# First unit's keys, queries and values evicted straight into attention's places

## The chip, the cores and the metric

The kernel runs on one core of one Trainium2 chip. The metric is the device time of one execution in microseconds (us); a kernel's time is the median of its runs.

## What is computed

The reference mixes two branches of the same 2048 x 640 input `x` in float32, with one gate per row:

```python
g = sigmoid((x * gate_w).sum(-1, keepdims=True))
qkv = x @ wqkv                   # 32 heads of 20, for q, k and v
idx = pos[:, None] - 2 * arange(8)[None, :]          # keys s, s-2, ..., s-14
logits = einsum("bhsd,bhswd->bhsw", q, k[idx]) * scale   # masked where idx < 0
a = (softmax(logits) applied to v[idx]) @ wo
b = irfft2(rfft2(x) * (w_r + 1j * w_i))
out = g * a + (1 - g) * b
```

The attention is local and dilated: row s looks at itself and at the seven rows before it with a step of two.

## The kernel before, in words

**Layout.** Row s of the input stands in partition s // 16 at place j = s % 16. Rows of even j and of odd j never meet in the attention, so the work has two parities (`par`), each with eight places `jj` (j = 2 jj + par). Eight consecutive places of one parity are in one partition, and the seven older keys that the first places need are in the partition in front. Columns are in four groups `hg` of 480: q, k and v of 160 columns each, and each of these in two halves `f` of 80 (`HC`, four heads of 20). A **unit** is u = 4 par + hg; one attention call `attend(par, h)` does half a unit, h = 2 hg + f.

**Projection** (`qkv`, lines 1038 to 1057). For each of the 64 combinations of place and group, fifteen matmuls (five blocks of 128 input columns, three terms of a high and low split) fill one PSUM bank with 480 columns; there are four such banks. Unit 0's first place has no split and takes five slower matmuls. ScalarE copies each bank into a tile `ev` (two places per tile), and each pair of places goes to a DRAM scratch `qkvd` (`store_rows`, line 1001). Units 0 and 4 store from SyncE's queue (SP), the others from ScalarE's. In the scratch, the rows of one column half are consecutive over all partitions.

**Attention** (`attend`, lines 1080 to 1115). `fetch` (line 1067) reads per half unit 15 consecutive key rows per partition into `kt` (seven of the partition in front, eight own), and eight query rows into `q`; `attend` reads the 15 value rows into `vt`. For units 0 and 4 all of these are on SP. Then, for each pair of places, `products` (line 1170) multiplies 2 x 8 x 80 elements of `kt` and `q` into `pr` and sums them in groups of 20 into the logits `L`. The multiplication is VectorE's, with the query first copied by ScalarE into a PSUM bank (`qbank`), except for some pairs that GpSimd does (`POOL_PR`; none in unit 0). Masks, maximum, exponential (ScalarE) and sums follow; GpSimd subtracts, scales and does the weighted products `pv`; VectorE reduces them to `o`, which goes to a second scratch `od`. `weigh`, `mask` and the rings of places `kv0` to `kv5`, `q0` to `q1`, `L0` to `L2`, `pr0`, `pr1` are shared by all half units. Unit 0's `ev` tiles use `ev0`, `ev1`, `pr0`, `pr1`.

**The rest.** Columns of `x` are folded (`fold`, on VectorE or GpSimd; folds 3 to 6 use the places `pv0`, `pv1` and are stored to DRAM), transformed by matmuls (`cols`, tiles `z`), multiplied in the frequency domain (`freq`, tiles a to d, `xa`, `xc`, `P`, `g`), transformed back (`spatial`, tiles oa to od, `ha`, `hb`); the output projection is `project_even` and `project_odd` (`woa`, `wob`, fifteen matmuls each). The low halves of the projection weights (`w<-raw,w`) and of the odd rows of `x` (`xo<-xt,xo`) are subtracted on GpSimd.

**What sets the order.** The program records all operations (`Plan.record`; every instruction is issued from one helper, so the trace gives it line 987) and orders them before anything is issued: a list schedule over estimated costs is repeated once per number in `STEPS`, each of which seeds random moves, and the list `MOVES` then takes single operations out of an engine's order and puts them at another place. Each engine and each DMA queue issues in that order. Units are taken in the order `UNITS` = (0,0), (0,1), (1,0), (1,1), (0,2), and so on, as (parity, half). `work` (line 857) records the stages.

Of the kernel before, what the change touches and what calls it, by code (L numbers as in the profile page):

```python
# [18 lines left out]
HD = 20  # L19
GORD = (1, 2, 3, 4, 5, 0) + tuple(range(6, 16))  # L20
GC = 160
HC = 80
# [127 lines left out]
class Plan:  # L150
# [394 lines left out]
)  # L545
MOVES = (
# [1085 lines left out]
```

## Time and profile before

| | us |
|---|---|
| median of 3 runs (lowest, highest) | 441.99 (441.64, 442.71) |
| the profiled execution | 443.3 |
| its span, from the first instruction to the last | 441.5 |
| TensorE, VectorE, GpSimd, ScalarE busy in the span | 428.1, 380.6, 353.5, 209.3 |

All is one profiled execution. A matmul's recorded end is modelled, and matmuls overlap, so a busy TensorE need not run at its peak. TensorE's clock was granted in full over the whole span. An idle stretch of an engine is put down to what it waited for last.

### The profile page before, as it was taken

Reading aid. Unit: us, or ns where it says so; the run is one execution under the profiler, and the core shown is the slowest. Engines: PE = TensorE matmul, PEld = TensorE weight load, DVE = VectorE, ACT = ScalarE, POOL = GpSimd, SP = SyncE. Lnnn points to the kernel's source line nnn. Section 1 sums busy time; section 2 is a strip of 40 time slices with the busy share of each in tenths; the row PEclk is TensorE's granted clock in tenths of the full one; section 3 lists DMA queues with packets and bytes.
Section 4 is the critical chain, followed back from the end, with each engine's and each line's share of the span. In section 5 each row is a group of like instructions: output and inputs, shape, how many; then the busy total and the mean of one; then the engine's idle time right before and its main releaser. Section 6 shows DMA issues by size and latency. Waiting matters only on the chain.

```text
span 441.5 us, 9185 instructions
## 1 busy us (share of the span) xinstructions
PE 428.1 (97%) x3501; PEld 372.5 (84%) x3501; DVE 380.6 (86%) x499; ACT 209.3 (47%) x551; POOL 353.5 (80%) x313
## 2 busy tenths in 40 slices
PE   4999999999999999999999999999999999999996
PEld 3788888888888888888888778798889899999996
DVE  2575089899999999999999999999999999989682
ACT  3574245242225223453235466666766876754310
POOL 1067876589999999798799967887488999876994
PEclk9999999999999999999999999999999999999999
DMA  8959998929676658999588677957843445443545
GB/s 296 379 172 344 333 351 276 355 80 322 199 204 210 186 162 223 322 303 305 180 244 240 193 235 256 314 193 250 313 136 91 117 118 149 76 58 112 148 91 117
DMA packets 83835, 95.52 MB, mean 216 GB/s; under 512 B 18104, under 2 KB 73528, under 8 KB 83792
## 3 DMA queue, kind: packets, MB, share of 16 engines
q1 hardware_dynamic: 53728, 68.39, 47.9%
q10 hardware_dynamic: 28848, 23.85, 18.0%
q0 software_dynamic: 1216, 2.71, 4.5%
q8 instruction: 27, 0.44, 0.4%
q14 instruction: 16, 0.13, 0.1%
HBM read 64.04 MB, written 30.89 MB: 215 GB/s over the span
## 4 chain that ended last, share of the span: by engine, by line
PE 78%; DVE 10%; DMA 4%; ACT 3%; issue 2%; POOL 1%; SPq 0%; ACTq 0%; DVEq 0%; POOLq 0%
PE qkv L987 44%; PE woa L987 7%; PE wob L987 7%; PE a L987 4%; PE g L987 3%; PE oa L987 2%; PE xa L987 2%; PE oTp L987 2%; DMA kt3a<-qkvd 2%; PE hb L987 2%; PE xc L987 1%; POOL pv6b L987 1%; DMA qkvd<-ev 1%; DVE o2a L987 1%; DVE pr3a L987 1%
## 5 line engine op out<-in xcount | busy, mean ns | idle before, releaser
L987 PE MATMUL qkv<-w,xo 128*128 128x480 f32 (+1 forms) x480 | 115.7, 386 | 0.7 <-ACT ev L987 0.7
L987 PE MATMUL qkv<-w,xe 128*128 128x480 f32 (+1 forms) x465 | 107.3, 382 | 0.0
L987 PEld LDWEIGHTS qkv<-w,xo 128*128 128x128 f32 x480 | 89.1, 188 | 18.1 <-ACT ev L987 2.4
L987 PEld LDWEIGHTS qkv<-w,xe 128*128 128x128 f32 x465 | 87.4, 188 | 14.8 <-ACT ev L987 0.6
L987 ACT COPY ev<-qkv 128x480 f32<-128x480 f32 x64 | 35.4, 562 | 74.6 <-PE qkv L987 67.9
L987 PE MATMUL woa<-wo,oT 128*128 128x320 f32 x240 | 44.5, 321 | 0.5 <-DVE oT L987 0.5
L987 PE MATMUL wob<-wo,oT 128*128 128x320 f32 x240 | 43.3, 319 | 0.0
L987 PEld LDWEIGHTS woa<-wo,oT 128*128 128x128 f32 x240 | 36.8, 188 | 2.2 <-DVE oT L987 1.4
L987 PEld LDWEIGHTS wob<-wo,oT 128*128 128x128 f32 x240 | 36.6, 188 | 1.4 <-ACT ya L987 0.4
L987 POOL TENSOR_TENSOR P<-X,wp 128x642 f32<-128x642 f32 x16 | 25.1, 1568 | 12.0 <-ACT X L987 12.0
L987 POOL TENSOR_TENSOR xo<-xt,xo 128x640 fp32r<-128x640 f32 x8 | 12.4, 1571 | 23.2 <-ACT z L987 23.2
L987 PEld LDWEIGHTS a<-bt,zg 32*128 32x128 f32 x160 | 22.1, 184 | 2.7 <-issue 1.7
L987 PE MATMUL a<-bt,zg 32*128 32x161 f32 x160 | 24.1, 300 | 0.0
L987 PE MATMUL b<-bt,zg 32*128 32x161 f32 x160 | 24.1, 300 | 0.0
L987 PE MATMUL d<-bt,zg 32*128 32x161 f32 x160 | 24.1, 300 | 0.0
L987 PE MATMUL c<-bt,zg 32*128 32x161 f32 x160 | 24.1, 300 | 0.0
L987 PE MATMUL oa<-gt,zj 32*128 32x160 f32 x160 | 24.0, 300 | 0.0
L987 PE MATMUL ob<-gt,zj 32*128 32x160 f32 x160 | 24.0, 300 | 0.0
L987 PE MATMUL oc<-gt,zj 32*128 32x160 f32 x160 | 23.8, 299 | 0.0
L987 PE MATMUL od<-gt,zj 32*128 32x160 f32 x160 | 23.8, 299 | 0.0
L987 PEld LDWEIGHTS oa<-gt,zj 32*128 32x128 f32 x160 | 21.9, 185 | 1.4 <-issue 1.1
L987 PEld LDWEIGHTS b<-bt,zg 32*128 32x128 f32 x160 | 22.1, 184 | 0.0
(303 smaller groups left out, 1246.8 us busy)
## 6 DMA issues: line engine op xcount, KB each, us to landing
qkvd<-ev ACTq DMA_DIRECT2D x24, 480.0 KB, 3.7
wp<-in_ws SPq DMA_DIRECT2D x16, 642.0 KB, 5.6
fx<-in_x SPq DMA_DIRECT2D x8, 640.0 KB, 6.9
qkvd<-ev SPq DMA_DIRECT2D x8, 480.0 KB, 5.9
raw<-in_wqkv SPq DMA_DIRECT2D x15, 240.0 KB, 4.1
xt<-in_xT SPq DMA_DIRECT2D x8, 320.0 KB, 8.4
fd<-fx SPq DMA_DIRECT2D x4, 640.0 KB, 6.6
mm<-in_t_mm SPq DMA_DIRECT2D x8, 320.0 KB, 3.8
```

The lines of the kernel that those rows point to most:

```text
L987: p.sp.dma_start(raw[:, c0:c1], src[:, c0:c1])
```

## The change

Unit 0 (`par` 0, `hg` 0) no longer goes through the scratch.

- `own` takes both halves' places `kt`, `vt`, `q` and `L` at the start and clears the seven front rows of partition 0 on VectorE.
- `keep` takes the place of the eviction: six copies of 80 columns per bank, straight to row 7 + jj of `kt` and `vt` and row jj of `q`. ScalarE makes four (values' come as numbers 4 and 5, on VectorE).
- After each second place it records products of the pair with the keys that are there in the partition itself: rows 7 - m to 7, that is 1, 3, 5 and 7 of 8 rows, for m = 0, 2, 4 and 6. For m = 2 and 4 GpSimd multiplies; VectorE does all reductions.
- After the last place, rows 8 to 14 of `kt` and `vt` go to rows 0 to 6 of the next partition by transfers within the on-chip memory, each in two pieces (112 and 15 partitions): eight transfers on SP.
- `attend` for the two halves fetches nothing and does the other 7, 5, 3 and 1 rows of the products, all on VectorE.
- Four stores and six fetches are gone. Unit 0's tiles `ev` are gone, and with them its use of `pr0` and `pr1` as such.
- `first_keys`, which nothing called, and the unused parameters `block`, `c0` are taken out.
- `STEPS` and `MOVES` are replaced: 374 seeds for 321, 2323 moves for 1897.

```diff
+KEEP_DVE = (4, 5)
...
-        self.evrs = {0: ring("ev0", "ev1", "pr0", "pr1"), 4: ring("e0", "e1", "ev0", "ev1")}
+        self.evrs = {4: ring("e0", "e1", "ev0", "ev1")}
...
-        self.fetched, self.ahead = {}, None
+        self.fetched, self.begun, self.ahead = {}, {}, None
+        self.own()
         self.qkv(0, 0)
...
+    def own(self):
+
+        for f in range(2):
+            nm = f"0{'ab'[f]}"
+            kt, vt = (self.kvr.next(f"{i}t{nm}", 15, HC) for i in "kv")
+            self.fetched[0, f] = kt, vt, self.qr.next(f"q{nm}", 8, HC)
+            self.begun[0, f] = self.Lr.next(f"L{nm}", 8, 4, 8)
+            for to in (kt, vt):
+                self.p.dve.memset(to[0:1, 0:7], 0.0)
+
+    def keep(self, b, jj):
 
         p = self.p
...
+        for n, f, i in ((0, 0, 2), (1, 0, 0), (2, 1, 2), (3, 1, 0), (4, 0, 1), (5, 1, 1)):
+            to = self.fetched[0, f][i][:, jj if i == 2 else 7 + jj]
+            (p.dve.tensor_copy if n in KEEP_DVE else p.act.copy)(to, b[:, HC * n : HC * n + HC])
+        if jj % 2:
+            p.chain = "logits"
+            for f in range(2):
+                kt, _, q = self.fetched[0, f]
+                m = jj - 1
+                self.products(kt, q, m, self.begun[0, f][:, m : m + 2], f"0{'ab'[f]}{m}o", m in POOL_OWN, 7 - m, 8)
+            p.chain = ""
+        if jj == 7:
+            for f in range(2):
+                for to in self.fetched[0, f][0:2]:
+                    for p0, p1 in ((1, 113), (113, 128)):
+                        p.sp.dma_start(to[p0:p1, 0:7], to[p0 - 1 : p1 - 1, 8:15])
...
-            if jj % 2 == 0:
-                ev = self.evrs.get(u, self.evr).next(f"ev{u}_{jj}", 6, 2, HC)
-            p.act.copy(ev[:, b0:, jj % 2], b[:, 0:n].rearrange("p (i c) -> p i c", c=HC))
+            if u == 0:
+                self.keep(b, jj)
+            else:
+                if jj % 2 == 0:
+                    ev = self.evrs.get(u, self.evr).next(f"ev{u}_{jj}", 6, 2, HC)
+                p.act.copy(ev[:, :, jj % 2], b[:, 0:480].rearrange("p (i c) -> p i c", c=HC))
...
-            if jj % 2:
-                self.store_rows(ev[:, b0:], u, b0, jj - 1)
+            if u and jj % 2:
+                self.store_rows(ev, u, jj - 1)
...
-        L = self.Lr.next(f"L{nm}", 8, 4, 8)
+        if (par, h) not in ((0, 0), (0, 1)):
+            (S if early else self.queue("vt")).dma_start(vt.rearrange("p a b -> p (a b)"), self.key_rows(par, h, 2, 0, 15), max_dma_last_dim=PACKET)
+        begun = (par, h) in self.begun
+        L = self.begun[par, h] if begun else self.Lr.next(f"L{nm}", 8, 4, 8)
         for jj in range(0, 8, 2):
-            self.products(kt, q, jj, L[:, jj : jj + 2], f"{nm}{jj}", jj in POOL_PR.get((par, h), ()))
+            pool = jj in POOL_PR.get((par, h), ())
+            self.products(kt, q, jj, L[:, jj : jj + 2], f"{nm}{jj}", pool, 0, 7 - jj if begun else 8)
...
-    def products(self, kt, q, jj, L, nm, pool):
+    def products(self, kt, q, jj, L, nm, pool, r0=0, r1=8):
...
+        pr = self.prr.next(f"pr{nm}", 2, 8, HC)[:, :, r0:r1]
+        w = kt[:, jj + r0 : jj + r0 + 8]
...
+POOL_OWN = (2, 4)
```

## Rows read from the trace of the kernel before

**Rows 1.** Stretches: length, busy per engine, granted clock, DMA share, GB/s.

```profile
0.00:10.00 10.00, 3.77 (x13) 3.14 (x14) 2.00 (x5) 3.36 (x5) 2.05 (x9) 1.00 0.81 284
10.00:171.00 161.00, 161.00 (x726) 136.41 (x725) 131.88 (x138) 60.92 (x168) 126.64 (x106) 1.00 0.80 253
...
238.00:345.00 107.00, 104.64 (x1119) 89.77 (x1121) 101.28 (x164) 69.14 (x183) 83.77 (x72) 1.00 0.66 215
...
437.00:441.50 4.50, 0.56 (x4) 0.30 (x3) 0.74 (x2) 0.00 (x0) 0.00 (x0) 0.99 0.47 122
sum 441.50, PE 428.14 PEld 372.54 DVE 380.63 ACT 209.34 POOL 353.46; mean PE 53.52 PEld 46.57 DVE 47.58 ACT 26.17 POOL 44.18
```

**Rows 2.** TensorE's waits: total us, times, longest.

```profile
PE warmed L987 <- DVE warm L987: 6.2, 1, 6.2
PE xa L987 <- ACT xd L987: 1.3, 2, 1.1
```

**Rows 3.** Chain of waits that ended last: start us, us, what.

```profile
9.16 162.10 PE qkv L987 x726
...
304.15 2.21 PE woa L987 x15
...
336.95 2.49 PE woa L987 x15
```

**Rows 4.** VectorE in order of time: start, us, what, idle before.

```profile
56.72 1.49 DVE L987 TENSOR_TENSOR pr0a<-kt0a,qbank 128x1280 f32<-128x1280 f32 x1 [16.39 <-ACT qbank L987]
...
62.55 2.88 DVE L987 TENSOR_REDUCE L0a<-pr0a 128x64 f32<-128x1280 f32 x2
...
74.04 0.41 DVE L987 TENSOR_REDUCE m0a<-L0a 128x32 f32<-128x256 f32 x1
74.37 2.87 DVE L987 TENSOR_TENSOR pr0b<-kt0b,qbank 128x1280 f32<-128x1280 f32 x2
...
80.54 1.43 DVE L987 TENSOR_TENSOR pr4a<-kt4a,qbank 128x1280 f32<-128x1280 f32 x1
```

**Rows 5.** ScalarE in order of time: start, us, what, idle before.

```profile
14.55 0.16 ACT L987 COPY z<-qkv 128x1 f32<-128x1 f32 x1 [3.33 <-PE qkv L987]
14.61 0.57 ACT L987 COPY ev<-qkv 128x480 f32<-128x480 f32 x1
...
38.35 0.61 ACT L987 COPY ev<-qkv 128x480 f32<-128x480 f32 x1
```

**Rows 6.** Two early stretches, same columns as rows 1.

```profile
20.00:40.00 20.00, 20.00 (x93) 17.10 (x93) 14.73 (x34) 12.93 (x31) 11.37 (x9) 1.00 0.80 256
40.00:57.00 17.00, 17.00 (x79) 14.65 (x78) 0.61 (x2) 4.87 (x16) 15.05 (x16) 1.00 1.02 336
```

**Rows 7.** GpSimd in order of time: start, us, what, idle before.

```profile
44.31 1.21 POOL L987 TENSOR_TENSOR w<-raw,w 128x480 fp32r<-128x480 f32 x1
...
62.58 2.41 POOL L987 TENSOR_TENSOR w<-raw,w 128x480 fp32r<-128x480 f32 x2 [2.10 <-ACT z L987]
...
87.27 5.51 POOL L987 TENSOR_TENSOR pv0a<-vt0a,L0a 128x640 f32<-128x640 f32 x4 [4.16 <-DMA fd<-fx]
...
105.05 2.96 POOL L987 TENSOR_TENSOR pr4b<-kt4b,q4b 128x1280 f32<-128x1280 f32 x1
```

**Rows 8.** DMA issues: count, KB each, median us from issue to landing.

```profile
qkvd<-ev ACTq DMA_DIRECT2D x24, 480.0 KB, 3.7
...
out<-ya SPq DMA_DIRECT2D x8, 320.0 KB, 2.4
...
kt0a<-qkvd SPq DMA_DIRECT2D x1, 600.0 KB, 6.6
...
vt0a<-qkvd SPq DMA_DIRECT2D x1, 600.0 KB, 10.5
```

**Rows 9.** TensorE in order of time: start, us, what.

```profile
37.37 19.67 PE L987 MATMUL qkv<-w,xo 128*128 128x482 f32 x89
...
66.98 1.25 PE L987 MATMUL qkv<-w,xo 128*128 128x482 f32 x5
```

More of the change, by code (lines that the diff above doesn't have):

```diff
@@ L999, in load_x, with store_rows @@
         p.chain = ""
-    def store_rows(self, src, u, block, jj):
+    def store_rows(self, src, u, jj):
         n, k = src.shape[1], src.shape[2]
@@ L1005, in store_rows @@
             tensor=d.tensor,
-            offset=d.offset + ((6 * u + block) * ROWS + 7 + jj) * HC,
+            offset=d.offset + (6 * u * ROWS + 7 + jj) * HC,
             ap=[[8 * HC, 128], [ROWS * HC, n], [1, k * HC]],
@@ L1009, in store_rows, with terms_qkv @@
         (self.p.sp if u in SP_STORES else self.p.act).dma_start(to, src.rearrange("p i j c -> p i (j c)"))
-    def terms_qkv(self, j, hg, c0, c1, whole):
+    def terms_qkv(self, j, hg, n, whole):
         hi, lo = self.xT[j]
@@ L1016, in terms_qkv @@
             if whole:
-                terms.append((self.xraw[j][:, x], self.wraw[hg, t][:, c0:c1]))
+                terms.append((self.xraw[j][:, x], self.wraw[hg, t][:, 0:n]))
             else:
-                terms += [(a[:, x], w[hg][t][:, c0:c1]) for a, w in ((hi, self.wh), (hi, self.wl), (lo, self.wh))]
+                terms += [(a[:, x], w[hg][t][:, 0:n]) for a, w in ((hi, self.wh), (hi, self.wl), (lo, self.wh))]
         return terms
-    def first_keys(self):
-        p = self.p
-        n = 2 * HC
-        kept = self.one("ev_first", 2, 8, HC, tag="pr1")
-        done = 0
-        for jj in range(8):
-            b = self.ps(BQ, f"qk0_{jj}")
-            terms = self.terms_qkv(2 * jj, 0, 0, n, jj == 0)
-            for i, (a, w) in enumerate(terms):
-                p.pe.matmul(b[:, 0:n], a, w, start=(i == 0), stop=(i == len(terms) - 1))
-            p.act.copy(kept[:, :, jj], b[:, 0:n].rearrange("p (i c) -> p i c", i=2))
-            if jj in FIRST_STORES:
-                self.store_rows(kept[:, :, done : jj + 1], 0, 0, done)
-                done = jj + 1
+    def own(self):
[7 more added lines that the diff above has]
+    def keep(self, b, jj):
+        p = self.p
+        for n, f, i in ((0, 0, 2), (1, 0, 0), (2, 1, 2), (3, 1, 0), (4, 0, 1), (5, 1, 1)):
[13 more added lines that the diff above has]
+                        p.sp.dma_start(to[p0:p1, 0:7], to[p0 - 1 : p1 - 1, 8:15])
     def qkv(self, par, hg, between=None):
@@ L1040, in qkv @@
         u = 4 * par + hg
-        b0 = 0
-        c0, n = b0 * HC, 480 - b0 * HC
         for jj in range(8):
@@ L1045, in qkv @@
             b = self.ps(BO if u == 7 and jj > 3 else BQ, f"qkv{u}_{jj}")
-            terms = self.terms_qkv(j, hg, c0, 482 if hg == 0 else 480, j == 0 and hg == 0)
+            terms = self.terms_qkv(j, hg, 482 if hg == 0 else 480, j == 0 and hg == 0)
             for i, (a, w) in enumerate(terms):
                 p.pe.matmul(b[:, 0 : w.shape[1]], a, w, start=(i == 0), stop=(i == len(terms) - 1))
-            if jj % 2 == 0:
-                ev = self.evrs.get(u, self.evr).next(f"ev{u}_{jj}", 6, 2, HC)
-            p.act.copy(ev[:, b0:, jj % 2], b[:, 0:n].rearrange("p (i c) -> p i c", c=HC))
+            if u == 0:
[4 more added lines that the diff above has]
+                p.act.copy(ev[:, :, jj % 2], b[:, 0:480].rearrange("p (i c) -> p i c", c=HC))
             if hg == 0:
-                p.act.copy(self.z[:, j : j + 1], b[:, n : n + 1])
-            if jj % 2:
-                self.store_rows(ev[:, b0:], u, b0, jj - 1)
+                p.act.copy(self.z[:, j : j + 1], b[:, 480:481])
+            if u and jj % 2:
+                self.store_rows(ev, u, jj - 1)
             if between:
@@ L1089, in attend @@
         kt, vt, q = self.fetched.pop((par, h), None) or self.fetch(par, h)
-        (S if early else self.queue("vt")).dma_start(vt.rearrange("p a b -> p (a b)"), self.key_rows(par, h, 2, 0, 15), max_dma_last_dim=PACKET)
-        L = self.Lr.next(f"L{nm}", 8, 4, 8)
+        if (par, h) not in ((0, 0), (0, 1)):
+            (S if early else self.queue("vt")).dma_start(vt.rearrange("p a b -> p (a b)"), self.key_rows(par, h, 2, 0, 15), max_dma_last_dim=PACKET)
+        begun = (par, h) in self.begun
+        L = self.begun[par, h] if begun else self.Lr.next(f"L{nm}", 8, 4, 8)
         for jj in range(0, 8, 2):
-            self.products(kt, q, jj, L[:, jj : jj + 2], f"{nm}{jj}", jj in POOL_PR.get((par, h), ()))
+            pool = jj in POOL_PR.get((par, h), ())
+            self.products(kt, q, jj, L[:, jj : jj + 2], f"{nm}{jj}", pool, 0, 7 - jj if begun else 8)
         for square in ((4, 1, 0, 1), (2, 4, 4, 2), (1, 2, 6, 4)):
@@ L1168, in key_rows @@
         )
-    def products(self, kt, q, jj, L, nm, pool):
+    def products(self, kt, q, jj, L, nm, pool, r0=0, r1=8):
         p = self.p
-        pr = self.prr.next(f"pr{nm}", 2, 8, HC)
-        w = kt[:, jj : jj + 8]
-        w = bass.AP(tensor=w.tensor, offset=w.offset, ap=[w.ap[0], [HC, 2], [HC, 8], [1, HC]])
+        pr = self.prr.next(f"pr{nm}", 2, 8, HC)[:, :, r0:r1]
+        w = kt[:, jj + r0 : jj + r0 + 8]
+        w = bass.AP(tensor=w.tensor, offset=w.offset, ap=[w.ap[0], [HC, 2], [HC, r1 - r0], [1, HC]])
         if pool:
@@ L1182, in products @@
             qj = qj.rearrange("p (j c) -> p j c", j=2)
-        mul(pr, w, qj.unsqueeze(2).broadcast_to([128, 2, 8, HC]))
+        mul(pr, w, qj.unsqueeze(2).broadcast_to([128, 2, r1 - r0, HC]))
         p.dve.tensor_reduce(
-            out=L.rearrange("p j h r -> p j r h"),
+            out=L[:, :, :, r0:r1].rearrange("p j h r -> p j r h"),
             in_=pr.rearrange("p j r (h d) -> p j r h d", d=HD),
@@ L1566 @@
 ON_SP = ((0, 0), (0, 1), (1, 0), (1, 1))
-FIRST_STORES = (3, 5, 7)
+POOL_OWN = (2, 4)
 POOL_PR = {(p, h): (6,) for p in range(2) for h in range(8) if (p, h) not in ((0, 0), (0, 1), (1, 0))}
```

513 rows, old and new, of tables (MOVES, STEPS) are left out of this document.

## The prediction

> **What bounds the kernel now.** I read first the busy times by stage: TensorE is busy for 428.1 of the span's 441.5 us, 97% [rows 1]. The stages and its waits say where the other 13.4 us lie. 6.2 us pass before its first matmul [rows 2], 3.9 us after its last one (0.56 us busy in the 4.5 us from 437.0 on), and nothing is idle from 10 to 171 us [rows 1]. That leaves 441.5 - 428.14 - 6.2 - 3.9 = **3.2 us**, 2.4 of them between 238 and 345 us (104.64 busy of 107) [rows 1], where its largest wait is for ScalarE's xd [rows 2]. Nothing in the change touches the start, the tail or the number of matmuls, so those 3.2 us are the plain room. A busy engine could still be a slow one, so I looked at the chain of waits: 726 qkv matmuls in 162.1 us are 0.223 us each, one unbroken stretch, and late in the kernel a group of fifteen woa matmuls takes 2.21 us in one place and 2.49 us in another [rows 3]. Some room is therefore hidden in the busy time: of the six woa groups of fifteen that this chain shows whole, two have the longer time. A third of 32 such groups at 0.28 us is an estimate of **3.0 us**.
>
> VectorE is the engine behind it. It is idle for 16.4 us before unit 0's first products at 56.7 us and does unit 4's first product at 80.5 us [rows 4]; from 238 to 345 us it is busy for 101.3 of 107 us [rows 1]. Its lead early on is what the change can buy, and TensorE's 3.2 us are what a lead can be exchanged for.
>
> **Part by part, against the profiled execution** (443.3 us, span 441.5; it lies 1.3 us above the median of 441.99, and I carry the differences over to the median).
>
> Evictions. Eight copies of 480 columns go, 0.57 us each (4.6 us); 48 of 80 columns come, 32 on ScalarE, 16 on VectorE. No row shows 80 columns from PSUM: below lies one column, 0.16 us, above 480 columns, 0.57 [rows 5]. On the line between them 80 columns take 0.23 us (estimate): 7.4 us, so ScalarE gains 2.8 us of work, with bounds of 32 x 0.16 - 4.6 = 0.5 and 32 x 0.57 - 4.6 = 13.6. ScalarE is busy for 12.9 of 20 us there [rows 6] and a bank is filled in 15 x 0.22 = 3.3 us with four banks in turn; the copies hold a bank some 0.5 us longer. I cost it at nothing; without that cover it is 8 x 0.5 = 4 us on TensorE.
>
> Products. VectorE's pitch is 1.40 us at 1280 elements (two in 2.88 us, the second's end) and 0.33 us at 256 (from 74.04 to 74.37, the next start) [rows 4], so 1.04 ns per element and 0.06 us. Own rows have 160, 480, 800 and 1120 elements a pair; two of the four multiplications go to GpSimd. VectorE does 3840 elements in 6 instructions per head, 4.4 us, 8.8 for both heads; the rest after the halo is 5120 elements in 8 instructions, 5.8 us, 11.6 for both. Before it was 16 x 1.40 = 22.4 us. The 16 copies on VectorE add 16 x 0.15 = 2.4 us (estimate by the same line; at most the 0.33 of 256 elements, 5.3 us). Sum for VectorE: -2.0 + 2.4 = +0.4 us, up to +3.3. Four clearing writes on one partition stand where VectorE is busy for 2.0 of 10 us [rows 1]: nothing. ScalarE's copies of the query rise from 8 to 12, four of at most the 0.57 us of 480 columns, hidden as above.
>
> GpSimd. Its product of 1280 elements takes 2.96 us [rows 7]; four of 480 and 800 elements, two each, come to 2 x (1.1 + 1.85) = **6.0 us** more, in a stretch where it is busy for 11.4 of 20 us and then 15.0 of 17 [rows 6]. This is the only part that may cost something, see below.
>
> Transfers. Four stores of 480 KB, four fetches of 600 KB and two of 320 KB go, 4.96 MB; eight pieces, 4 x 127 x 2240 bytes = 1.14 MB, come. The DMA engines are full there (share 1.02, 336 GB/s from 40 to 57 us) [rows 6], so 3.8 MB frees 11 us of link time. All of it stands in SP's queue; ten fewer and eight more issues change that queue by about 1 us, and the weight loads behind them come sooner, not later. The new pieces wait for the last eviction on SP; behind them are loads that TensorE needs some 15 us later.
>
> When the halo is there. The last eviction was made at 38.35 us, 0.61 us long [rows 5]; with the longer copies it ends at 39.4. The eight issues follow at once. No row shows a transfer from one partition of the on-chip memory to the next: below lies the shortest landing, 2.4 us, above that of vt0a, 10.5 us; I take kt0a's 6.6 us for the first, since it is issued in the same full stretch [rows 8]. The first late product then starts at **46 us** (42 to 50) and not at 56.7. VectorE has 5.3 free us from 20 to 40 [rows 6] for 8.8 + 2.4 us of early work, so it runs on to about 46 as well: the two meet. Unit 0's logits are done at 46 + 11.6 + 1 = 59 us instead of 80.5: **21 us ahead**.
>
> The order. Both lists of numbers from which the issue order is made are new, so every queue may be ordered otherwise, far from unit 0 too. No row prices that; I take it that the new order uses what lead there is, and (B) and (D) are the cases in which it does not.
>
> What is late next. Unit 4 follows on VectorE. Its matmuls start at 37.4 us and the last of them ends at 68.2 (66.98 + 1.25) [rows 9]; store and fetch take 3.7 + 6.6 us by the medians, 2.4 + 2.4 at the least [rows 8]. So its keys cannot be there before 73 to 78 us, whatever VectorE has done. Unit 0's weighted sums do not fill the hole before that: GpSimd's first, pv0a, is made at 87.3 us after a wait for the store of a fold from the same place [rows 7]. Of 21 us some **3 to 8 us of lead** remain (estimate: 80.5 - 78 and 80.5 - 73).
>
> What the lead buys. TensorE's stalls are single waits of up to 1.3 us in sum per kind [rows 2], all smaller than such a lead. I take 2.5 of the 3.2 us as recovered: the 2.4 between 238 and 345 us, and 0.1 elsewhere. 443.3 - 2.5 = 440.8 for such an execution, **439.5 us** at the median. 0.3%, which is 1.3 us, is about what a measurement of this kernel can tell from no change.
>
> **Rivals.**
> (B) The hole only moves. VectorE waits at 60 us for unit 4 as it waited at 40 for unit 0, and the stalls after 238 us come from the chain ScalarE xd to TensorE xa, which has its own order. For it: the xa wait [rows 2], and the bound of 73 to 78 us above. Against it: VectorE is nearly full from then on, so any lead is kept. Time: a tenth of the 3.2 us less, 441.99 - 0.3 = 441.7 us.
> (C) The hidden seams close too: 3.2 + 3.0 = 6.2 us, 435.8 us. For it: groups of equal work with unequal times [rows 3]. Against it: the lead is small beside the 330 us that follow. The Trainium skill (Perfetto Trace Analysis, Identifying the Most-Contended Engine) says that matmul busy time is a poor measure and that the busy share of weight loads should be used; that is 84% here (372.54 of 441.5 us), which by the rule would leave up to 70 us. In the trace the stretch with no gap at all has weight loads busy for 136.4 of 161 us, 85% [rows 1], so 84% is full pace and I take no more than (C) from it.
> (D) Slower: GpSimd's 6.0 us push the low parts of the second unit's weights. The first of them is made at 44.3 us, the fifth ends at 65.0 (62.58 + 2.41) [rows 7]; TensorE's last matmul with odd rows, its only other work, ends at 68.2 [rows 9]. The slack is 3.2 us; beyond it TensorE stands still, for 6.0 - 3.2 = 2.8 us: 441.99 + 2.8 = 444.8 us. It decides as soon as GpSimd's order puts all four products before those parts. Against it: folds stand there too, which may be put behind.
> (E) The halo comes late. Rows show transfers that follow each other closely; were every piece to pay its full landing in turn, with 2.4 us [rows 8] eight of them need 19 us, from 39.4 to 58.6, no sooner than the 56.7 of today, and only the own half is gained: VectorE is ready at 58.6 + 11.6 = 70, still before unit 4's keys. Time: 441.7 us. The Trainium skill (DMA: Bandwidth & Descriptors, Rules for kernel authors) speaks so against this change: pieces under 64 KB are mostly overhead, and two transfers to disjoint partitions serialize; by its fixed 2.0 us a piece the eight end at 55 us.
>
> **How the numbers follow.** Forecast 0.46, (B) 0.20, (C) 0.14, (D) 0.12, (E) 0.08. Faster by over 0.3%: forecast and (C), 0.60; within: (B) and (E), 0.28; slower: (D), 0.12. The range runs from (C) to past (B) and (E) with the 1.1 us by which the three runs differ: 435.7 to 442.8. It leaves out (D), 0.12, and some tails. Forecast and (C) are both faster; their own range is 435.7 to 440.6.
>
> **What would show it.** Right: the first late product near 46 us, VectorE's gap before it short, a new gap before unit 4's first product, that product 3 to 8 us sooner, TensorE's idle time between 171 and 390 us down from 3.2 to under 1 us, an unchanged start and tail. Wrong: an idle TensorE between 60 and 75 us (D), late products near 57 us (E), idle time from 238 to 345 us still 2.4 us (B), or a unit 4 that starts as early as unit 0 ends, which would make more of the lead than I do.

## The result, and the profile after

The changed kernel takes **447.38 us** (447.03 to 448.92), the kernel before beside it 442.35 (441.64 to 443.35): ratio 1.0116, 95% interval 1.0096 to 1.0136. The forecast was 439.5. The profiled execution took 447.61 us, its span 445.8.

The same stretches of the changed kernel as in [rows 1] (length, busy time of TensorE, its weight loads, VectorE, ScalarE and GpSimd, granted clock, DMA share, GB/s), and two more:

```profile
0.00:10.00 10.00, 7.64 (x20) 4.91 (x21) 5.89 (x11) 4.81 (x7) 2.05 (x9) 1.00 0.82 301
10.00:171.00 161.00, 160.86 (x759) 136.52 (x757) 140.57 (x169) 63.70 (x199) 140.09 (x114) 1.00 0.77 238
171.00:210.00 39.00, 36.34 (x359) 30.73 (x359) 34.95 (x38) 16.67 (x44) 28.27 (x23) 0.96 0.77 258
...
238.00:345.00 107.00, 101.99 (x1046) 87.17 (x1045) 97.84 (x161) 67.29 (x179) 83.45 (x71) 1.00 0.66 215
345.00:390.00 45.00, 43.20 (x649) 39.77 (x648) 42.84 (x52) 31.60 (x81) 35.50 (x34) 1.00 0.36 87
...
437.00:445.80 8.80, 5.47 (x37) 5.21 (x36) 1.65 (x3) 0.00 (x0) 0.96 (x2) 0.98 0.20 74
sum 445.80, PE 430.50 PEld 373.59 DVE 385.74 ACT 210.99 POOL 360.15; mean PE 53.81 PEld 46.70 DVE 48.22 ACT 26.37 POOL 45.02
```

The span is 4.3 us longer, and these rows say where, for TensorE: idle time in the first 10 us 2.4 instead of 6.2 (-3.9), in the tail 3.3 instead of 3.9 (-0.6), between 10 and 437 us 9.6 instead of 3.2 (**+6.4**), and 2.4 us more of busy time (430.50 against 428.14). So there is a gain at the start, where I had expected none, and a larger loss, all of it behind 171 us: until then TensorE is as full as before.

TensorE's waits in the changed kernel (total us, times, longest), against [rows 2]:

```profile
PE qkv L988 <- ACT ev L988: 2.7, 1, 2.7
PE qkv L988 <- DMA st<-in_w: 1.3, 1, 1.3
PE woa L988 <- DVE oT L988: 1.3, 2, 0.9
PE warmed L988 <- DVE warm L988: 1.1, 1, 1.1
PE g L988 <- DVE s L988: 1.0, 1, 1.0
PE xc L988 <- ACT X L988: 1.0, 1, 1.0
PE ha L988 <- ACT ho L988: 0.9, 1, 0.9
PE oTp L988 <- DVE oT L988: 0.7, 2, 0.4
PE xa L988 <- DVE s L988: 0.7, 1, 0.7
PE oTp L988 <- ACT ya L988: 0.7, 1, 0.7
PE ha L988 <- ACT os L988: 0.2, 1, 0.2
PE xa L988 <- ACT xd L988: 0.2, 1, 0.2
```

The two waits for the warm tile and for st belong to the start. The other ten lines are twelve waits behind 171 us, 9.4 us in all; the kernel before has 2.8 there, the 1.3 for xd of [rows 2] and these:

```profile
PE qkv L987 <- ACT ev L987: 0.7, 2, 0.5
PE woa L987 <- DVE oT L987: 0.5, 2, 0.3
PE xa L987 <- issue: 0.3, 1, 0.3
```

No single one explains the loss: the largest is 2.7 us, for a ScalarE copy, and the rest are of 0.2 to 1.0 us in the frequency stage, the transform back and the output projection, which the text of the change doesn't touch.

Unit 0 itself went nearly as forecast. VectorE in order of time (start, us, what, idle before), against [rows 4]:

```profile
0.84 0.17 DVE L988 MEMSET warm<- 128x128 f32 x1 [0.84 <-PEq L1691]
...
45.03 1.32 DVE L988 TENSOR_TENSOR pr0a<-kt0a,qbank 128x1120 f32<-128x1120 f32 x1
...
65.02 0.32 DVE L988 TENSOR_REDUCE L0b<-pr0b 128x8 f32<-128x160 f32 x1
...
75.47 2.88 DVE L988 TENSOR_TENSOR pr4a<-kt4a,qbank 128x1280 f32<-128x1280 f32 x2 [6.19 <-DMA kt4a<-qkvd]
```

The first late product is at 45.03 us (forecast 46), the logits are done at 65.3 (forecast 59), a gap of 6.19 us for unit 4's keys follows, and unit 4 starts 5.1 us sooner (80.54 to 75.47; forecast 3 to 8). The first row is the surprise: VectorE clears the warm tile, which the first matmuls read, as its first instruction. In the kernel before that stood behind a cast that waited for a load:

```profile
5.48 0.49 DVE L987 CAST xe<-st 128x640 fp32r<-128x640 f32 x1 [5.48 <-DMA st<-in_xT]
5.95 0.17 DVE L987 MEMSET warm<- 128x128 f32 x1
```

So TensorE began at 6.2 us [rows 2]; now it begins at 1.1 and its first qkv is at 5.29 us instead of 9.16 [rows 3].

**The wait at 185 us.** ScalarE and then VectorE of the changed kernel there:

```profile
184.39 0.57 ACT L988 COPY zg<-z 128x512 f32<-128x512 f32 x1
187.11 0.30 ACT L988 COPY qbank<-q3b 128x160 f32<-128x160 f32 x1 [2.15 <-issue]
187.34 0.55 ACT L988 COPY ev<-qkv 128x480 f32<-128x480 f32 x1
```

```profile
185.56 1.48 DVE L988 TENSOR_TENSOR pr3a<-kt3a,qbank 128x1280 f32<-128x1280 f32 x1
```

ScalarE is idle for 2.15 us before it copies a query into `qbank`. The profile names no releaser; but that copy starts as VectorE's product pr3a (185.56 + 1.48 = 187.04 us) ends, which reads the bank. Behind it in ScalarE's order stands the eviction `ev`, for which TensorE stood still from 185.3 to 187.9. Short stretches of the changed kernel right there show a second price:

```profile
185.00:188.00 3.00, 0.34 (x7) 0.10 (x3) 2.97 (x3) 0.89 (x3) 3.00 (x3) 1.00 0.86 276
188.00:190.00 2.00, 2.00 (x8) 1.42 (x8) 2.00 (x3) 0.88 (x3) 2.00 (x2) 0.86 0.45 163
190.00:192.00 2.00, 2.00 (x19) 1.80 (x20) 2.00 (x2) 0.00 (x0) 1.92 (x3) 0.50 0.03 8
192.00:194.00 2.00, 2.00 (x27) 1.83 (x24) 2.00 (x2) 1.20 (x4) 2.00 (x2) 0.79 0.15 38
```

After the idle time the granted clock falls to 0.50 (1.2 GHz) and is back in full at 194 us: 2 x (0.14 + 0.50 + 0.21) = 1.7 us of TensorE's pace. The group of 40 z matmuls that starts at 190.20 us takes 3.68 us, the one at 182.88 took 2.40. This loss is in the busy time; that it is most of the 2.4 us added there is not shown, since join170 below has 1.6 us more than the kernel before without any slow clock.

### The profile page after: what moved, and what is told of

Read it like the earlier page. It is cut to its first block, busy times and chain, and to the rows that moved or that the text cites. A ratio compares the mean times of both kernels' runs of the same rounds, so it can differ in the third digit from the quotient of the medians.

```text
span 445.8 us, 9235 instructions
## 1 busy us (share of the span) xinstructions
PE 430.5 (97%) x3501; PEld 373.6 (84%) x3501; DVE 385.7 (87%) x531; ACT 211.0 (47%) x579; POOL 360.1 (81%) x317
## 4 chain that ended last, share of the span: by engine, by line
PE 77%; DVE 14%; ACT 5%; issue 3%; DMA 1%; ACTq 0%; DVEq 0%
PE qkv L988 45%; PE woa L988 7%; PE wob L988 5%; PE z L988 3%; PE oa L988 3%; PE a L988 2%; PE g L988 2%; DVE xd L988 2%; PE ha L988 2%; DVE prl L988 2%; PE xa L988 2%; PE hb L988 2%; PE oTp L988 1%; DVE s L988 1%; PE xc L988 1%
## 5 line engine op out<-in xcount | busy, mean ns | idle before, releaser
L988 PE MATMUL qkv<-w,xo 128*128 128x480 f32 (+1 forms) x480 | 113.9, 386 | 2.7 <-ACT ev L988 2.7
L988 PE MATMUL qkv<-w,xe 128*128 128x480 f32 (+1 forms) x465 | 106.2, 382 | 0.1
L988 ACT COPY ev<-qkv 128x480 f32<-128x480 f32 x56 | 31.0, 561 | 70.6 <-PE qkv L988 64.9
L988 ACT CAST oT<-oTp 128x384 fp32r<-128x384 f32 (+1 forms) x32 | 13.4, 428 | 22.1 <-PE woa L988 7.5
```

The lines of the kernel that those rows point to most:

```text
L988: p.dve.memset(w, 0.0)
```

## The experiments

Every kernel here issues the operations in an order written out in full; that part of the edit is the same in all:

```diff
-        order = self.order()
-        if MOVES:
-            order = self.settle(self.moved(order))
+        order = self.settle({e: [self.ops[i] for i in ORDER[e]] for e in ENGS})
```

`ORDER` holds the order of one of the two kernels, or of one up to a time and of the other behind it, with the moves named below.

### Which half of the order costs it

**join70** and **join170**: the changed kernel, all of it, in its own order to about 70 and 170 us; behind that the order of the kernel before. **rev170**: the reverse, the kernel before in its own order to 170 us, then in the changed kernel's; unit 0 goes through the scratch.

> The changed kernel with its own order for everything issued in about the first 70 us (unit 0 whole, 594 of 4145 operations) and, behind that, every engine and queue in the relative order of the kernel before. Theory 1 (the loss sits in the new order far behind unit 0): in the changed kernel TensorE is some 2.5 us of work ahead of before from 20 to 180 us and loses 2.9 us in one wait at 185 us and about 5 between 280 and 380 us; with the old order behind 70 us those waits go, so 439 to 442 us against 442.4 before. Theory 2 (the unit's new work itself costs it: GpSimd's 6 us, the small copies): the old order doesn't help, 445 to 448 us.

> As the other joined order, but the changed kernel's own order is kept to about 170 us, just ahead of the wait at 185 us. Theory 1: the lead of 2.5 us (TensorE) and 8 us (VectorE, GpSimd) stands at 170 us and the old order follows, so 438.5 to 442 us. Theory 2: 445 to 448 us. If only the order between 70 and 170 us were at fault, this one would be slow and the one joined at 70 us fast.

> The reverse: the kernel before, with its stores and fetches for unit 0, in its own order to about 170 us, and behind that every engine and queue in the relative order of the changed kernel. Nothing of the change is in it but the order of the later part. Theory 1: TensorE loses the same 7 us behind 170 us as the changed kernel does (lead +2.4 at 170 us, -4.7 at 430 us), without the lead of 2.4 us at the start: 446 to 450 us. Theory 2: 441 to 444 us, like before.

| kernel | us (lowest to highest) | ratio to before, 95% interval |
|---|---|---|
| before, same chip | 442.62 (440.58 to 443.82) | |
| join70 | 440.43 (439.67 to 441.53) | 0.9950 [0.9931, 0.9969] |
| join170 | 439.74 (439.44 to 440.81) | 0.9941 [0.9923, 0.9959] |
| rev170 | 454.85 (454.54 to 455.55) | 1.0283 [1.0254, 1.0311] |

The change with the old order behind 170 us beats both kernels; the new order behind 170 us without the change is 12 us slower than before. So the loss of 447.38 - 439.74 = 7.6 us is in the order behind 170 us and not in unit 0. TensorE's waits in join170, start aside:

```profile
PE xa L922 <- ACT xd L922: 1.3, 2, 1.1
...
PE woa L922 <- DVE oT L922: 0.5, 2, 0.3
PE xa L922 <- issue: 0.3, 1, 0.3
```

These are those of the kernel before [rows 2]: behind 171 us 2.5 us in all, against 9.4 in the changed kernel. The two profiled executions are 6.9 us apart (447.61 and 440.67): TensorE's idle time by 6.2 us (15.3 against 9.1) and its busy time by 0.7. The waits are the loss; the 1.7 us of slow clock can't simply be added to them.

rev170 is 5 us slower than the 446 to 450 that theory 1 gave it. It has the later order's waits (ev 2.5 us, and eleven of 6.8 us behind 238 us), and near the place where its orders meet two for zg that neither kernel has. TensorE's waits for zg in sum, then ScalarE:

```profile
PE z L969 <- ACT zg L969: 3.3, 2, 3.1
```

```profile
178.57 0.22 ACT L969 COPY L2b<-low 1x16 f32<-1x16 f32 x1 [3.77 <-DVE L2b L969]
```

ScalarE waits 3.77 us for VectorE, and behind that copy stands zg, for which TensorE waits; the granted clock is 0.91 from 171 to 210 us. In the changed kernel VectorE is some 8 us further by then (its sum o1b that follows L2b is at 170.14 us, in rev170 at 178.45), the same copies stand in the same order, and TensorE doesn't wait. Of the 454.85 - 447.38 = 7.5 us between the two the early start (below) is 2.7 to 2.9. So in the new later order VectorE's lead may be worth the other 4.6 us; that the joint itself makes these waits is not ruled out. rev170 shows the sign of the loss and not its size.

### One wait, or many

**fix185**: the changed kernel in its own order, with one ScalarE operation three places earlier.

```diff
 ScalarE, from 184 us:
+    ev6_0 <- qkv6_1
     L3a <- low
     zg <- z4_0
     qbank <- q3b        (waits for VectorE)
-    ev6_0 <- qkv6_1
```

**join245**, **join200**, **join300**: as join170, with the change of orders at about 245, 200 and 300 us. In the expectations of these four, theory 1 is a single wait with its echo, theory 2 many waits, theory 3 a lead eaten anywhere.

> The changed kernel's own order with one operation moved: on ScalarE the copy of the eviction ev6_0 (second place of unit 6) stands three places earlier, ahead of the copy of the query into qbank that waited 2.15 us for VectorE at 185 us. Theory 1 (a single wait starts the loss, and what follows at 190 to 360 us is its echo): the whole loss behind 180 us goes, TensorE keeps the 2.4 us by which it led at 170 us; about 440.5 us. Theory 2 (the later order loses in several places, each by itself): only this wait goes, 447.4 - 2.7 = 444.7 us, TensorE's wait for ScalarE's ev is gone from the first place of its list, and it is again some 2 us behind the kernel before at 320 us. Theory 3 (the lead is eaten by whatever comes next, as VectorE is the real bound there): 447 us, another wait of 2 to 3 us within 20 us of the first.

> The changed kernel's own order up to about 245 us, then the order of the kernel before. TensorE was 0.7 us behind the kernel before at 245 us in the changed kernel, and 2.4 us ahead at 170. The order to 200 us and the one to 300 us added waits of their own at the place of the change of orders; this place lies between two stages. Theory 2 (each wait of the new order costs itself and nothing follows): 439.7 + 3.1 = 442.8 us, TensorE's waits behind 245 us those of the kernel before (xa for ScalarE's xd 1.3 us). Echo of the one wait at 185 us (theory 1): 446 us.

> The changed kernel's own order up to about 200 us, so with the wait at 185 us, then the order of the kernel before. TensorE loses 4.2 us between 170 and 200 us in the changed kernel (2.4 ahead to 1.8 behind). Theory 2 (the loss sits where the order is the new one): 439.7 + 4.2 = 443.9 us, no further loss behind 200 us. Theory 1 says the same up to 200 us but expects the echo too: 446 to 447 us.

> The changed kernel's own order up to about 300 us, then the order of the kernel before. TensorE is 2.2 us behind the kernel before at 300 us in the changed kernel and was 2.4 ahead at 170. Theory 2: 439.7 + 4.6 = 444.3 us, the last 2.5 us of the loss (300 to 360 us) gone. Theory 1 (echo): 447 us.

| kernel | us (lowest to highest) | ratio to before, 95% interval |
|---|---|---|
| fix185 | 445.53 (444.62 to 446.14) | 1.0074 [1.0055, 1.0092] |
| join245 | 443.76 (441.32 to 445.09) | 1.0027 [1.0008, 1.0046] |
| join200 | 446.13 (445.43 to 446.41) | 1.0087 [1.0070, 1.0104] |
| join300 | 446.69 (446.31 to 446.86) | 1.0100 [1.0085, 1.0115] |

TensorE's waits in fix185, start aside:

```profile
PE woa L922 <- DVE oT L922: 1.3, 2, 0.9
...
PE z L922 <- ACT zg L922: 1.1, 1, 1.1
...
PE xc L922 <- ACT X L922: 1.1, 1, 1.1
PE g L922 <- DVE s L922: 1.1, 1, 1.1
```

The moved copy gives 447.38 - 445.53 = 1.85 us back: the `ev` wait is gone, the clock stays at 1.00, and a wait of 1.1 us for the next ScalarE copy behind the same `qbank` copy has taken part of its place. Behind 238 us the same waits come 1.5 to 1.9 us earlier: eleven of 6.7 us in the changed kernel, eleven of 7.1 here, and eleven of 6.8 in rev170, which has no change in unit 0. So there is no echo; they don't come from the wait at 185 us but are the later order's own (theory 2, 0.8 us above its figure). What makes each of the eleven was not taken apart.

join245 agrees, 1 us above theory 2's figure: from 439.74 to 443.76 is 4.0 us for the order up to 245 us, and 3.6 us more, to 447.38, for the rest. join200 and join300 lie 2.2 to 2.4 us above theory 2 and at the times of theory 1 (446 to 447 us). They don't speak for an echo, though: where their orders meet, each waits longer than either order does there alone (join200 twice for `ev` at 202 and 207 us, 0.65 us each, where the kernel before has one wait of 0.54; join300 1.6 us for oT at 303 us, where the changed kernel has 0.4), and behind that join200 has the waits of the kernel before. With such waits added they tell little about the split.

### The gain at the start, and the worth of VectorE's lead

**warm**: the kernel before with only the clearing of the warm tile moved to the head of VectorE's order. **start12**: the kernel before with the first 12 us of every engine in the changed kernel's order (63 operations). **latewarm**: join170 with the cast of xe and the warm tile back in the order of the kernel before.

```diff
 VectorE in join170:          in latewarm:
-    warm
     vt0b, kt0a, vt0a, kt0b (cleared)
+    xe <- st
+    warm
     w0_2 <- st, w0_2
     w0_0 <- st, w0_0
-    xe <- st
```

> The kernel before with one instruction moved: VectorE clears the tile for the warm-up matmuls first and not behind the conversion that waits for a load until 5.5 us. The changed kernel does this too, and its first matmuls start 3 to 4 us sooner. If TensorE's work is the bound of the whole kernel, the 2.4 to 3.3 us that this gave there carry to the end: 439 to 440 us. If VectorE's chain is the bound later, they are lost on the way: 441.5 to 442.5 us.

> The changed kernel's order up to about 170 us and then that of the kernel before (which took 439.74 us), but with VectorE's cast of xe and its clearing of the warm tile in the order of the kernel before, so that TensorE's first matmul is again at about 6.2 us and its first qkv at about 9.2 instead of 5.5. It separates the two halves of that gain. If the gain of 2.9 us comes from VectorE's lead behind unit 0: 439.7 to 440.2 us. If it comes from the earlier start: 439.74 + 2.0 (TensorE's lead at 20 to 170 us is 2.0 us) = 441.7 us, up to 442.6.

> The kernel before, with only the first 12 us of all engines in the changed kernel's order (63 operations; warm tile cleared first, first qkv at 5.5 to 7 us instead of 9.2); unit 0 as before. If the earlier start alone makes the gain: 442.5 - 2.0 to 2.9 = 439.6 to 440.5 us. If the earlier start is kept only where VectorE has its lead behind unit 0 (the warm tile alone moved forward gave 442.15 against 442.62): 442 us, and TensorE's lead of some 2 us at 40 us is gone again before 400.

| kernel | early start | unit 0 changed | us (lowest to highest) | ratio to before, 95% interval |
|---|---|---|---|---|
| join170 | yes | yes | 439.74 (439.44 to 440.81) | 0.9941 [0.9923, 0.9959] |
| latewarm | no | yes | 442.63 (442.31 to 443.22) | 1.0008 [0.9998, 1.0017] |
| start12 | yes | no | 439.82 (437.91 to 440.94) | 0.9928 [0.9903, 0.9952] |
| warm | only the tile | no | 442.15 (440.78 to 443.81) | 0.9997 [0.9979, 1.0015] |

Read in pairs: with or without the early start, unit 0's new way is worth nothing that can be measured as long as the old order follows behind 170 us (439.74 against 439.82, 442.63 against 442.3 for the kernel before in that comparison). The early start is worth 2.7 to 2.9 us with either (442.51 for the kernel before beside start12). In latewarm unit 4's first product is at 78.88 us, 1.7 us sooner than before, and VectorE has done 143.6 us of work by 171 us where the kernel before had done 133.9; 4.2 of the difference are added work, so its lead is 5.5 us. TensorE's waits behind 171 us are nonetheless those of [rows 2]; there is one of 0.8 us more at 27 us, for a copy of z among unit 0's evictions. Its first two lines, and VectorE at 180 us:

```profile
PE warmed L974 <- DVE warm L974: 5.7, 1, 5.7
PE xa L974 <- ACT xd L974: 1.3, 2, 1.1
```

```profile
180.30 0.42 DVE L974 TENSOR_REDUCE m2b<-L2b 128x32 f32<-128x256 f32 x1 [3.37 <-ACT L2b L974]
```

This is where most of the lead goes. ScalarE's copies of L2b stand behind copies zg, and those waited 2.75 us for TensorE, which is full; so VectorE waits for TensorE's pace by way of ScalarE. At 238 us 0.4 us of the lead is left, by the same count of work done. No run here has another order behind 170 us that is made for the lead, so the result says what the lead is worth in this order, not in every one.

That warm alone brings nothing doesn't fit start12. TensorE's first qkv, start12 and then warm:

```profile
5.45 1.95 PE L917 MATMUL qkv<-st 128*128 128x482 f32 x2 [1.46 <-DMA st<-in_w]
```

```profile
7.08 1.94 PE L917 MATMUL qkv<-st 128*128 128x482 f32 x2 [3.08 <-DMA st<-in_w]
```

In warm's order it waits for a later load, so only a part of the start is gained. But the profiled execution of warm took 440.82 us, near the lowest of its ten runs; why the others are longer the one trace can't show, and it stays open.

### Two parts of the change taken apart

**noown**: join170 without products between evictions. **onepiece**: join170 with each transfer between partitions whole.

```diff
 noown
-        if jj % 2:
+        if False:
...
-            self.products(kt, q, jj, L[:, jj : jj + 2], f"{nm}{jj}", pool, 0, 7 - jj if begun else 8)
+            self.products(kt, q, jj, L[:, jj : jj + 2], f"{nm}{jj}", pool, 0, 8)
 onepiece
-                    for p0, p1 in ((1, 113), (113, 128)):
+                    for p0, p1 in ((1, 128),):
```

> The order of the kernel of 439.74 us (the changed kernel's to 170 us, then that of before), without the products with own keys between the evictions: the four pairs of both halves are done whole, after the transfers between partitions. Nothing is left out. VectorE does 16 x 1.40 = 22.4 us after the halo instead of 11.6 plus the remnants, GpSimd 6.0 us less. If VectorE's lead behind unit 0 is lost in the gap before unit 4 anyway (6.9 us until 77.0 us): unit 0's logits at some 68 us, 439.7 us, no difference. If that lead is worth something: unit 4's first product later by up to 4 us and 441 to 443 us.

> As the kernel of 439.74 us, but each of the four transfers between partitions is one piece of 127 partitions instead of two of 112 and 15. The two pieces landed in 2.3 to 3.1 us. If the number of pieces is what counts: the same or 1 us sooner for the halo, 439.7 us. If a piece of 127 partitions is moved by one of the sixteen engines (estimate: 127 x 2240 bytes at a sixteenth of the 336 GB/s seen from 40 to 57 us is 13.5 us): the landing of each is 13 us or more, the first late product at 54 us or later instead of 45.8, unit 0's logits at 75 us or later, time 440 to 450 us, by how far unit 4's products are pushed beyond 77 us. The Trainium skill (DMA: Bandwidth & Descriptors, the section on why a DMA increments its semaphore by 16 and not by 1) has the rule for the second case.

noown: 445.36 us (444.86 to 446.62), ratio 1.0075 [1.0050, 1.0100], slower than either theory said. Unit 4's first product comes some 4 us later, as the second theory had it (81.14 against 76.99 us), but TensorE loses sooner than that: it is busy for only 16.8 of the 20 us from 60 to 80, at a granted clock of 0.91. ScalarE there, and then TensorE:

```profile
61.80 0.30 ACT L922 COPY qbank<-q0b 128x160 f32<-128x160 f32 x1 [2.15 <-DVE pr0b L922]
...
62.53 0.15 ACT L922 COPY z<-qkv 128x1 f32<-128x1 f32 x1
```

```profile
62.73 1.17 PE L922 MATMUL qkv<-w,xe 128*128 128x480 f32 x2 [2.57 <-ACT z L922]
```

It is the wait of 185 us again: a `qbank` copy that waits for a late VectorE product holds up the copies behind it that empty TensorE's bank. With that, noown doesn't say what the products with own keys are worth by themselves; it says that in this order VectorE may not be late.

onepiece: **479.47 us** (478.02 to 481.35), ratio 1.0842 [1.0801, 1.0883]. A stretch and VectorE's first late product:

```profile
58.00:60.00 2.00, 0.00 (x0) 0.00 (x0) 0.00 (x0) 0.00 (x0) 0.00 (x0) 1.00 0.07 25
```

```profile
66.97 1.32 DVE L922 TENSOR_TENSOR pr0a<-kt0a,qbank 128x1120 f32<-128x1120 f32 x1 [21.04 <-DMA kt0a<-kt0a]
```

From 48 to 66 us the DMA engines are busy for 0.07 to 0.10 of their time, about one of sixteen, at 24 to 33 GB/s. kt0b's piece was issued at 40.5 us and kt0a's behind it; the product that needs kt0a starts at 67.0, so they took some 13.2 us each, if they moved one after the other (13.5 were expected for one). VectorE waits 21.04 us. ScalarE, whose next query copy waits for VectorE's product, makes no eviction meanwhile, and the weight loads stand behind these pieces in SP's queue (TensorE waits 16.8 us for `ev`, 6.1 for z and 7.4 for the weights' low parts), so that no compute engine has work from 58 to 66 us. The expected 440 to 450 us counted unit 4's products alone and left this out. The Trainium skill (DMA: Bandwidth & Descriptors, Why a DMA increments its semaphore by 16 and not by 1) gives the rule: a transfer is spread over the largest number of engines, up to 16, that divides its count of partitions, and 127 gives one. The trace agrees: 0.07 of the time of sixteen engines is about one. So the cut at 112 and 15 in the change is not a detail.

## Why the prediction was wrong

**The step that failed is "The order".** It said: "No row prices that; I take it that the new order uses what lead there is". join170 shows that the new order costs 7.6 us behind 170 us, rev170 that it costs it without the change too, and fix185 that it does so by many waits of its own (one of 2.7 us, eleven of 6.7) in stages that the change doesn't touch. I named the two new lists as able to reorder every queue and then gave that a price of zero with no lower end. (B) and (D), which I called the cases in which the order doesn't help, held a loss of at most 2.8 us, at 60 to 75 us and none behind 171. A row did bear on it: the kernel before has 3.2 us of idle time between start and tail [rows 1], so another order could take away at most that much waiting, and nothing bounded what it could add.

In sum, against 442.4 us before: 2.7 to 2.9 us less for the early start, nothing measurable for unit 0, and 7.6 us more for the later order.

**"What the lead buys" failed too.** 2.5 of TensorE's 3.2 us were to be recovered. In latewarm and join170 the stalls are unchanged (xa for xd 1.3 us; 104.62 and 104.49 busy of 107 us from 238 to 345, 104.64 before [rows 1]). VectorE's lead doesn't get that far: in latewarm 5.5 us of it are there at 171 us and 0.4 at 238, lost while VectorE waits for ScalarE. For unit 0 alone, with the old order behind it, rival (B), no change, was right; its hole before unit 4 is there (6.19 us), but part of the lead outlived it, by 100 us.

**"Nothing in the change touches the start" was wrong**, with a gain of 2.7 to 2.9 us (join170, start12). The early start explains why join170 lands at 439.74, beside the 439.5 of the forecast: the number is right there by luck, for another reason.

The steps for unit 0 held in the main:

- Evictions hid: TensorE is busy for 160.86 of 161 us from 10 to 171 (in latewarm one wait of 0.8 us shows). Copies of 80 columns take 0.23 to 0.24 us in the median on ScalarE, as worked out (0.23); on VectorE they are recorded with 0.23 us too and follow each other after 0.15 to 0.16, where 0.15 had been worked out.
- GpSimd's added work was 6.0 us and is 6.7 (360.15 - 353.46); rival (D), that it would hold up the weights, fell with TensorE's full stretch. (D) had the right sign and the wrong mechanism.
- VectorE's was 0.4 and is 5.1 us (385.74 - 380.63). By recorded durations the clearing writes, costed at nothing, are 2.1 us (0.53 each), the sixteen copies 3.8 instead of 2.4, and the products with their sums save 0.8 instead of 2.0.
- The logits were done at 65.3 us and not at 59 because VectorE had not finished the early work at 45 us. Between 45.03 and 65.34 it still does 3.6 us of the second half's own rows and two parts of a fold, and it waits 2.4 us for ScalarE. The gap for unit 4's keys covered that.
- The halo was sooner than worked out: the pieces land 2.3 to 4.4 us after their issue, not 6.6, so rival (E) fell. The times to landing of kt0a's two pieces and then of kt0b's in the changed kernel:

```profile
DMA to landing us min/median/max: 2.3/2.6/2.8
```

```profile
DMA to landing us min/median/max: 2.9/3.7/4.4
```

kt0a's second piece was there at 44.60 us. VectorE came to it without idle time, so that the first late product at 45.03 was set by VectorE's early work, the other of the two that were to meet at 46. The eight issues didn't follow at once: seven went out between 39.55 and 46.53 us, the last, for vt0b, at 65.9, long before its use.

The first piece of kt0b (112 partitions), issued at 39.55 us, landed at 42.44, that of kt0a (15 partitions), issued at 40.27, at 42.59: 0.15 us apart and not one landing time behind the other. The seven were all there at 50.97 us, after 11.4 us, while their landing times add up to 20.1. The Trainium skill (DMA: Bandwidth & Descriptors, Rules for kernel authors) says that two transfers to disjoint partition halves serialize, because they share the same engines. Whether the data of these pieces moved in turn no row shows; the times to landing overlapped. Rival (C) found no support: TensorE's busy time didn't fall (428.14 us before, 430.50 after, 428.06 in latewarm).

## What to carry to other kernels

When a change comes with a new order of everything, split it before you explain it: the new code in the old order and the old code in the new order took two runs here and showed where the loss is. The place where two orders meet can add waits of its own, as in rev170, join200 and join300, so read the waits before the time. An engine that works in the listed order and serves two others (here ScalarE, with query copies that wait for VectorE and evictions that TensorE waits for) passes one engine's lateness to the other; look there first when the bound engine begins to wait. And on an engine that is full from its first matmul on, compare what stands ahead of that matmul: 3 us at the start were worth more here than 5 us of lead of the second engine, which was gone before it could be used.

## What the hardware showed that I had not expected

- The idle stretch of TensorE at 185 us cost more than its length: after 2.66 us without matmuls at 185 us the granted clock was 0.86, 0.50 and 0.79 in the next three stretches of 2 us (1.2 GHz in the middle one). With the wait cut to 1.1 us in fix185, in two parts, it stayed at 1.00.
- Transfers of 127 partitions in place of 112 and 15 made the kernel 40 us slower, at 25 GB/s where 336 had been seen [rows 6].
- Transfers from one partition to the next landed in 2.3 to 4.4 us, some as fast as the output's 320 KB stores of the kernel before, 2.4 us [rows 8]. Pieces of 112 partitions (251 KB) took 2.7 to 4.1 us, pieces of 15 (34 KB) 2.3 to 4.4.
